# Delaying the issue of the first K tile until VectorE's first constant is written, and letting GpSimd instead of SyncE wait for the output stores

## Chip, cores and metric

The kernel runs on one core of one Trainium2 chip. The metric is the device time of one execution in microseconds (us). A "span" is the length of the profiled part of an execution, from the first to the last instruction of the program on the core; it leaves out what happens around the program and is here 1.7 to 3 us shorter than the device time.

## The reference

Two independent attention decode blocks, A and B, are computed and their outputs concatenated. One block:

```python
# B, Sq, D = 8, 1, 1024 ; H, Sk, Dh = 32, 4096, 128 ; all bf16
q = (x @ wq).reshape(B, Sq, H, Dh).transpose(0, 2, 1, 3)
scores = jnp.einsum("bhqd,bhkd->bhqk", q, k_cache) * (Dh ** -0.5)
p = softmax(scores, axis=-1)
o = jnp.einsum("bhqk,bhkd->bhqd", p, v_cache)
y = o.transpose(0, 2, 1, 3).reshape(B, Sq, H * Dh) @ wo
# ... the same for B; result = concatenate([a, b], axis=-1)
```

There is one query token for each batch entry, so every byte of the K and V caches is read once and used once. The caches, weights and inputs are 1107 MB, and the output is 32 KB.

## The kernel before

All large loads go through a ring of three 8.4 MB slots in SBUF. A plan fixes the order of the loads and the slot of each: `wq` of block A, then K tile 0, then `wq` of block B, then K and V tiles in turn, and the two `wo` at the end. Every large load is issued by SyncE ("sp"), and each waits until the previous tenant of its slot has been used.

```python
plan = [("wq", 0, 1), ("k", 0, 0), ("wq", 1, 2)]          # (kind, number, slot)
for n in range(NQ - 1):
    plan.append(("k", n + 1, (n + 1) % 2))
    plan.append(("v", n, 2))
plan += [("v", NQ - 1, NQ % 2), ("wo", 0, 2), ("wo", 1, (NQ - 1) % 2)]
tenant = [None, None, ("x", 0)]                           # slots 0 and 1 start empty, x is in slot 2
# ...
def load_tiles():
    while issued[0] < len(plan):
        kind, n, w = plan[issued[0]]
        prev = before[issued[0]]                          # the tile that was in this slot
        dep = opUse.get(prev)                             # its last use
        if prev is not None and dep is None:
            return
        # ... dma(to, from_, key, [dep]) by kind ...
        issued[0] += 1
```

The first two loads wait for nothing and are emitted ahead of the block in which the engines branch off to their own streams. Two small loads of `x` (16 KB each) are issued by ScalarE; they wait for `c_oh`, VectorE's first constant. TensorE transposes `x`, and with that and `wq` it computes the queries. After the last store SyncE waits until all the output has landed.

```python
c_oh = add("dve", lambda e: e.tensor_copy(own_h[:], own), [c_own])
# ...
op_x = [dma(x_sb[:, c, :], caches[c][0].rearrange("b s d -> b (s d)"), ("x", 0), [c_oh], "act") for c in range(NC)]
# ... emit_xT: 16 small transposes of x on TensorE ...
op_xT = opUse[("x", 0)] = add("pe", emit_xT, [c_ident, op_x[-1]])
load_tiles()
# ...
P.run("sp", nc.sync, sems, part=(0, 2))
block = es.enter_context(nc.Block())

@block.sync
def _(eng):
    P.run("sp", eng, sems, part=(2, None))
    eng.wait_ge(sems[("out", 0)], counts[("out", 0)])
# ... tensor, scalar, vector ...
@block.gpsimd
def _(eng):
    P.run("pool", eng, sems)                              # writes constants, then has nothing to do
```

## Time and profile before

| | before |
|---|---|
| device time, median of 3 (range) | 2564.32 us (2564.31 to 2564.78) |
| span of the profiled execution | 2563.2 us |
| SyncE's DMA queue (q1) busy | 99.9% of the span |
| bytes read, mean rate | 1107.33 MB, 432 GB/s |
| VectorE (DVE) busy | 85% |

These lines are from the page of the kernel before: the busy time of the engines, the rate of the DMA in 40 equal slices, the busiest queue, the bytes and the engines of the chain that ended last.

```profile
span 2563.2 us, 18707 instructions
...
PE 1122.2 (44%) x7648; PEld 395.1 (15%) x7648; DVE 2173.1 (85%) x1043; ACT 130.0 (5%) x401; POOL 2.6 (0%) x14
...
GB/s 425 427 438 430 437 431 437 431 437 431 436 432 436 431 437 430 438 430 438 430 438 429 438 430 438 429 437 431 437 431 436 432 436 432 434 433 434 433 435 391
...
q1 hardware_dynamic: 19488, 1107.32, 99.9%
...
HBM read 1107.33 MB, written 0.03 MB: 432 GB/s over the span
...
DMA 52%; DVE 28%; issue 16%; PE 4%; another core or an unknown queue 0%; ACT 0%; DVEq 0%; SPq 0%
```

The queue's 99.9% and the even rate say that the 16 DMA engines have work from start to end; counted from the packet records, they are at least 99.4% busy in every stretch of 10 us between 10 and 2550 us. The chain of waits puts 52% on DMA and 28% on VectorE, but that does not make VectorE a second bound. A load waits for a free slot and so for the engine that used it, and the chain follows such a wait even though, by that count, the DMA engines were busy with other loads. The last slice (391) is clearly low: it holds the tail, after the last weights have landed. The first (425) holds the head, before the first bytes arrive; the second, at 427, is nearly as low, and why was not looked into. The packet records show 64 KB packets, 16 at a time, the first of them at 1.84 us; in full flow one takes 2.42 us.

Next, the start in the timeline of the kernel before. The columns are start in us, length in us, engine (a "q" marks work of the engine's sequencer, here the issue of a DMA), source line, operation, output and input, count, and in brackets how long the engine had been idle and what ended it.

```profile
0.81 0.41 SPq L208 DMA_DIRECT2D ring<-in_A_wq_dram  x1
...
1.27 0.42 SPq L208 DMA_DIRECT2D ring<-in_A_k_cache_dram  x1
...
2.29 0.17 DVE L225 CAST own_h<-own_m 128x8 bf16<-128x8 f32 x1 [2.29 <-POOL own_m L212]
...
2.50 0.59 ACTq L208 DMA_DIRECT2D ring<-in_A_x_dram  x1
...
15.97 1.10 PE L450 MATMUL misc<-ident,ring 8*128 8x8 bf16 x16 [15.97 <-DMA ring<-in_B_x_dram]
...
23.23 3.59 PE L284 MATMUL o<-ring,xT 128*8 128x512 bf16 x32 [6.15 <-DMA ring<-in_A_wq_dram]
...
43.72 4.42 DVE L329 TENSOR_TENSOR ring<-ring,qbc 128x8192 bf16<-128x8192 bf16 x1 [10.04 <-DMA ring<-in_A_k_cache_dram]
```

K tile 0 (K0) is issued 0.46 us after `wq`, but the multiply that needs it starts 20.5 us after the first use of `wq` (43.72 against 23.23 us). TensorE has `x` at 15.97 us and then waits 6.15 us for `wq`. The first K multiply waits for K0 itself, until 43.72 us. So `x` is not what the start waits for, and K0's issue at 1.27 us seems far too early to decide anything.

Finally, the instructions of the end barrier of the kernel before, from the listing of that source line. The columns are line, engine, operation, count, least, median and longest duration in ns, and the times in us of the first and last.

```profile
L162 POOLq EVENT_SEMAPHORE  x2: 17/17/17, 2563.0 to 2563.1; - x2
L162 POOLq DRAIN  x1: 349/349/349, 3.8 to 3.8; - x1
...
L162 SPq COMPARE_BRANCH  x1: 33/33/33, 2562.8 to 2562.8; - x1
L162 SPq DRAIN  x1: 7/7/7, 2563.0 to 2563.0; - x1
```

SyncE's branch at 2562.8 is what follows its wait for the output. GpSimd's own drain took place at 3.8 us and lasted 349 ns.

### The profile page before, as it was taken

The page shows a single profiled execution, that of the slowest core. Times are in us where ns is not written, and L with a number is a line of the kernel's source. Part 1 is how long each engine was busy: PE and PEld are TensorE (multiplying, and loading weights), DVE is VectorE, ACT ScalarE, POOL GpSimd, SP SyncE. Part 2 cuts the span into 40 slices and gives each one's busy share as a digit, 9 for nine tenths or more (in the row PEclk, how much of TensorE's full clock was granted, in tenths as well). Part 3 has the DMA queues.
Part 4 walks back from the last instruction along what each step waited for, and adds up shares of the span by engine and source line. Part 5 has one row for each costly group of instructions (what it writes and reads, how often), then busy time and mean ns, then how long its engine had stood idle before and what let it go on. Part 6 is the DMA issues. An engine that isn't in the chain of part 4 may idle for free.

```text
span 2563.2 us, 18707 instructions
## 1 busy us (share of the span) xinstructions
PE 1122.2 (44%) x7648; PEld 395.1 (15%) x7648; DVE 2173.1 (85%) x1043; ACT 130.0 (5%) x401; POOL 2.6 (0%) x14
## 2 busy tenths in 40 slices
PE   2443443443444444444444444443434444434435
PEld 1111111111111111111111111111111111111112
DVE  3898898898898898898898888888988988988983
ACT  1100000000000000000000000000000000000000
POOL 0000000000000000000000000000000000000000
PEclk7666675766667676766767666767767667666667
DMA  9999999999999999999999999999999999999999
GB/s 425 427 438 430 437 431 437 431 437 431 436 432 436 431 437 430 438 430 438 430 438 429 438 430 438 429 437 431 437 431 436 432 436 432 434 433 434 433 435 391
DMA packets 19577, 1107.49 MB, mean 432 GB/s; under 512 B 2224, under 2 KB 2272, under 8 KB 2416
## 3 DMA queue, kind: packets, MB, share of 16 engines
q1 hardware_dynamic: 19488, 1107.32, 99.9%
q8 instruction: 6, 0.10, 0.0%
q10 hardware_dynamic: 80, 0.05, 0.0%
q14 instruction: 3, 0.02, 0.0%
HBM read 1107.33 MB, written 0.03 MB: 432 GB/s over the span
## 4 chain that ended last, share of the span: by engine, by line
DMA 52%; DVE 28%; issue 16%; PE 4%; another core or an unknown queue 0%; ACT 0%; DVEq 0%; SPq 0%
DMA ring<-in_A_k_cache_dram 25%; DMA ring<-in_B_k_cache_dram 25%; DVE ring L329 10%; DVE ring L334 10%; PE red L344 4%; DVE s_sb L352 4%; DVE PM L369 3%; DMA ring<-in_B_wo_dram 1%; DVE rmax L358 1%; DVE rtmp L359 0%; ACT PM L290 0%; DVEq L135 0%; DVE ngm L362 0%; PE proj L432 0%
## 5 line engine op out<-in xcount | busy, mean ns | idle before, releaser
L329 DVE TENSOR_TENSOR ring<-ring,qbc 128x8192 bf16<-128x8192 bf16 x256 | 1131.8, 4421 | 311.3 <-DMA ring<-in_A_k_cache_dram 153.5
L344 PE MATMUL red<-ring,ident 128*128 128x512 bf16 x2048 | 784.0, 552 | 1390.3 <-DVE ring L334 1390.3
L334 DVE TENSOR_TENSOR ring<-ring 128x4096 bf16<-128x4096 bf16 x256 | 582.4, 2275 | 0.0
L344 PEld LDWEIGHTS red<-ring,ident 128*128 128x128 bf16 x2048 | 240.1, 128 | 1842.3 <-DVE ring L334 1492.9
L352 DVE TENSOR_REDUCE s_sb<-red 128x64 f32<-128x1024 f32 x256 | 312.1, 1219 | 3.7 <-PE red L344 3.7
L381 PE MATMUL pv<-ring,PM 128*32 128x512 bf16 x4096 | 274.8, 416 | 4.7 <-DVE PM L369 4.7
L369 DVE TENSOR_TENSOR PM<-pe,own_h 128x2048 bf16<-128x2048 bf16 x64 | 146.2, 2285 | 0.7 <-ACT pe L364 0.7
L381 PEld LDWEIGHTS pv<-ring,PM 128*32 128x32 bf16 x4096 | 104.2, 104 | 188.9 <-issue 116.7
L318 ACT ACTIVATE qbc<-misc 128x128 bf16<-128x128 f32 x64 | 17.8, 278 | 1093.7 <-PE misc L316 1093.7
L364 ACT ACTIVATE pe<-s_sb,ngm 128x256 bf16<-128x256 f32 x64 | 32.6, 509 | 467.4 <-DVE ngm L362 467.4
L389 ACT ACTIVATE accS<-pv 128x512 bf16<-128x512 f32 x64 | 38.2, 597 | 351.2 <-PE pv L381 351.2
L398 PEld LDWEIGHTS o<-accS,E 128*32 128x32 bf16 x1024 | 31.3, 100 | 49.6 <-issue 48.4
L398 PE MATMUL o<-accS,E 128*32 128x32 bf16 x1024 | 38.1, 185 | 0.7 <-ACT accS L389 0.7
L404 ACT ACTIVATE o_sb<-o 32x32 f32 (+1 forms) x64 | 11.9, 186 | 453.4 <-PE o L398 445.3
L358 DVE TENSOR_REDUCE rmax<-s_sb 128x1 f32<-128x256 f32 x64 | 26.9, 420 | 2.2
L437 DVE CAST orow<-proj 40x512 bf16<-40x512 f32 (+1 forms) x2 | 1.1, 554 | 26.1 <-PE proj L432 26.1
L432 PE MATMUL proj<-ring,on_sb 128*8 128x256 bf16 (+1 forms) x192 | 14.8, 387 | 13.6 <-DMA ring<-in_A_wo_dram 7.9
L311 ACT ACTIVATE qst<-qT 128x128 bf16 (+1 forms) x64 | 18.8, 293 | 2.0 <-DVE qT L304 2.0
L304 DVE COPY qT<-misc 128x64 bf16<-128x64 bf16 x8 | 3.5, 436 | 17.2 <-PE misc L300 17.2
L359 DVE TENSOR_SCALAR rtmp<-half,rmax 128x32 f32<-128x32 f32 x64 | 15.5, 241 | 2.3
L362 DVE TRANSPOSE_TENSOR_REDUCE ngm<-rtmp 128x1 f32<-128x32 f32 x64 | 13.6, 212 | 2.2
L316 PE MATMUL misc<-ident,qst 128*128 128x128 bf16 x64 | 14.8, 232 | 0.9 <-ACT qst L311 0.9
(33 smaller groups left out, 63.6 us busy)
## 6 DMA issues: line engine op xcount, KB each, us to landing
ring<-in_B_wo_dram SPq DMA_DIRECT2D x2, 3072.0 KB, 31.4
ring<-in_B_wo_dram SPq DMA_DIRECT2D x1, 1536.0 KB, 38.1
ring<-in_A_k_cache_dram SPq DMA_DIRECT2D x32, 39.9
ring<-in_A_v_cache_dram SPq DMA_DIRECT2D x32, 27.8
ring<-in_B_k_cache_dram SPq DMA_DIRECT2D x32, 39.9
ring<-in_B_v_cache_dram SPq DMA_DIRECT2D x32, 27.8
ring<-in_B_wo_dram SPq DMA_DIRECT2D x1, 512.0 KB, 38.9
out_dram<-orow SPq DMA_DIRECT2D x2, 4.0 KB
```

Of the source, the lines that this page charges most:

```text
L311: return e.activation(qst[:, n % 2, :].rearrange("p (j m) -> p j m", m=MP), from_.unsqueeze(2).to_broadcast([128, HQ, MP]), ACTF.Copy)
L318: opQbc[n] = add("act", lambda e: e.activation(qbc[:, n % 2, :], misc[:, 0:Dh], ACTF.Copy), [opQb[n], _at(opMul, NR * (n - 2) + NR - 1)])
L329: opMul[s] = add("dve", lambda e: e.tensor_tensor(v, v, qbc[:, n % 2, :].unsqueeze(1).to_broadcast([128, CT, Dh]), ALU.mult), [opT[("k", n ...
L334: return add("dve", lambda e: e.tensor_tensor(v[:, :, 0:64], v[:, :, 0:64], v[:, :, 64:128], ALU.add), [opMul[s]])
L344: i = e.matmul(dst, ident[:], v[:, g, :, j, :], start=(j == 0), stop=(j == 3))
L352: opRed[s] = add("dve", lambda e: e.tensor_reduce(s_sb[:, n % 2, r * CT:(r + 1) * CT], red_ps[s % 2][:, :].rearrange("p (t w) -> p t w", w ...
L358: m = add("dve", lambda e: e.tensor_reduce(rmax[:], s_sb[:, n % 2, :], AX.X, ALU.max), [opRed[NR * n + NR - 1]])
L364: opExp[n] = add("act", lambda e, at: e.activation(pe[:], s_sb[:, n % 2, :], ACTF.Exp, bias=ngm[:, n % 2:n % 2 + 1], scale=scale, accum_ou ...
L369: opPM[n] = add("dve", lambda e: e.tensor_tensor(PM[:], pe[:].unsqueeze(2).to_broadcast([128, T, HQ]), own_h[:].unsqueeze(1).to_broadcast( ...
L381: i = e.matmul(pv_ps[32 * q:32 * (q + 1), :], PM[:, t:t + 4, :].rearrange("p t j -> p (t j)"), v[:, t * Dh:(t + 4) * Dh], start=(g == 0), ...
L389: opAcc[n] = add("act", lambda e: e.activation(accS[:], pv_ps[:], ACTF.Copy), [opPV[n], _at(opExt, n - 1)])
L398: x = e.matmul(to, E[:, i, PH - 1 - u:PH - 1 - u + MB], accS[:, i * 128 + H * u:i * 128 + H * (u + 1)], start=(i == 0 and u == 0), stop=(i ...
```

## The change

K0 gets the wait for `c_oh` that the loads of `x` have. That puts its issue after the branch into the engines' own streams, so only `wq` stays ahead of it. The final wait moves from SyncE to GpSimd, which has been idle since the start and collects the end barrier.

```diff
-                dep = opUse.get(prev)
+                dep = c_oh if (kind, n) == ("k", 0) else opUse.get(prev)
...
-        P.run("sp", nc.sync, sems, part=(0, 2))
+        P.run("sp", nc.sync, sems, part=(0, 1))
         block = es.enter_context(nc.Block())
 
         @block.sync
         def _(eng):
-            P.run("sp", eng, sems, part=(2, None))
-            eng.wait_ge(sems[("out", 0)], counts[("out", 0)])
+            P.run("sp", eng, sems, part=(1, None))
...
         @block.gpsimd
         def _(eng):
             P.run("pool", eng, sems)
+            eng.wait_ge(sems[("out", 0)], counts[("out", 0)])
```

## The prediction

> **What bounds the kernel now.** The DMA stream. The queue table of the page has SyncE's queue (q1) busy for 99.9% of the span: 1107.32 MB at 432 GB/s. The costliest groups show VectorE (85% busy, not the limit) idle 311.3 us before the K multiply, mostly for K tiles. SyncE's own waits are for free buffers (V slots 1967.0 us, K slots 436.1 us), but loads are issued well before the stream needs them: K lands 39.9 us and V 27.8 us (median) after issue, while one 8.4 MB tile takes about 19 us at that rate (estimate). So 8 to 20 us of work is always queued. In the packet records the stream runs unbroken from the first packet at about 1.8 us to about 2559 us.
>
> **What the change does.**
> 1. The first K load moves from 1.27 us (timeline) to after VectorE's own_h copy (2.29 us, 0.17 long): about 1.2 us later. The wq load ahead of it still issues at 0.81 us and lands 22.3 us later, so K0 queues with about 20 us to spare and its data still follow wq without a gap. On the critical path: 0.
> 2. K0 now issues in the same moment as ScalarE's x loads (2.50 and 3.12 us), which wait for the same constant. The Trainium skill ("Perfetto Trace Analysis", HWDGE DMA instruction) says an issuer locks the descriptor generator, so one may delay the other by about an issue (0.3 to 0.4 us here). Perhaps x was meant to go ahead of K0. But x has landed by 15.9 us, and the query projection waits for wq until 23.2: 6.2 us of slack. "DMA: Bandwidth & Descriptors" (Queues, rings and completion order) says queues take turns by packet; this trace agrees: x's 2 KB packets ran at 7.3 and 12.2 us between wq's 64 KB packets, so they already pass K0. Worth 0.
> 3. The final wait moves to GpSimd. SyncE's wait ended at 2562.81, its branch and drain were done by 2562.99, GpSimd (which gathers the end barrier) went on at 2563.01, and the last engine left at 2563.19. With GpSimd waiting itself, one hop (0.03 to 0.1 us) goes, but GpSimd's drains took 0.19 and 0.35 us at the start against SyncE's 0.007. Net -0.1 to +0.3 us, all on the critical path.
>
> Bytes, order of loads in SyncE's queue, compute and loops are unchanged.
>
> **Predicted time:** 2564.4 us, range 2562.9 to 2566.0. Faster by over 2%: 0.005; within 2%: 0.99; slower by over 2%: 0.005.
>
> **What the profile should show.**
> - K0's issue at 2.4 to 3.2 us; x issues 0 to 0.5 us later, landing within 1 us of 15.9 or some us earlier; query projection still at about 23.2 us, first K multiply at 43.7 us (within 0.5).
> - q1 still 99.9%, 432 GB/s; VectorE's idle time unchanged.
> - GpSimd waits for the output stores; from their landing to the last instruction 0.3 to 0.7 us, as against 0.4.
>
> **What would make it wrong.** If x had been stuck behind K0's descriptors, it would land several us earlier: still no gain, since wq gates. If the stream ran dry near 21 us, the first K multiply would start late: I expect none. The 16 DMA engines finish the last weights some 2 us apart, so a different spread of small packets could move the end by about 1 us either way. [...] A change of 2% (51 us) would need another DMA rate throughout, which nothing here touches.

## The result, and the profile after

| | before | after |
|---|---|---|
| device time, median of 6 | 2564.48 us | 2564.87 us |
| range of the 6 | 2564.31 to 2564.78 | 2564.4 to 2565.95 |
| span of the profiled execution | 2563.2 us | 2563.0 us |

The ratio is 1.0002 with a 95% interval of 0.9989 to 1.0015. A ratio is the mean time of one kernel's runs over that of the other's of the same rounds, so it is not quite the ratio of the medians. The change made no difference that can be told from noise: the medians differ by 0.39 us, and the interval is about 3 us wide on either side. The spans of the six executions of the changed kernel were 2562.7 to 2563.2 us; what device time has beyond the span varied from 1.7 to 2.9 us among them, so most of the spread lies outside the span.

The same lines of the page, of the kernel after:

```profile
span 2563.0 us, 18707 instructions
...
PE 1120.7 (44%) x7648; PEld 394.1 (15%) x7648; DVE 2172.8 (85%) x1043; ACT 129.8 (5%) x401; POOL 2.5 (0%) x14
...
GB/s 425 427 438 430 437 431 437 431 437 431 437 431 436 432 436 431 435 433 435 432 436 431 436 431 437 431 436 432 434 434 434 433 433 435 433 434 434 434 434 392
...
q1 hardware_dynamic: 19488, 1107.32, 99.9%
...
HBM read 1107.33 MB, written 0.03 MB: 432 GB/s over the span
```

The first ten slices agree to the digit, although K0 is issued later in the first of them. The start, in the timeline of the kernel after:

```profile
0.80 0.40 SPq L208 DMA_DIRECT2D ring<-in_A_wq_dram  x1
...
2.28 0.17 DVE L225 CAST own_h<-own_m 128x8 bf16<-128x8 f32 x1 [2.28 <-POOL own_m L212]
...
2.48 0.35 SPq L208 DMA_DIRECT2D ring<-in_A_k_cache_dram  x1
2.49 0.59 ACTq L208 DMA_DIRECT2D ring<-in_A_x_dram  x1
...
15.87 1.11 PE L450 MATMUL misc<-ident,ring 8*128 8x8 bf16 x16 [15.87 <-DMA ring<-in_B_x_dram]
...
23.15 3.19 PE L284 MATMUL o<-ring,xT 128*8 128x512 bf16 x32 [6.17 <-DMA ring<-in_A_wq_dram]
...
43.47 4.42 DVE L329 TENSOR_TENSOR ring<-ring,qbc 128x8192 bf16<-128x8192 bf16 x1 [10.30 <-DMA ring<-in_A_k_cache_dram]
```

K0 is issued 1.21 us later, and `x`, the query projection and the first K multiply start where they did, within 0.25 us. And the end barrier of the kernel after:

```profile
L162 POOLq EVENT_SEMAPHORE  x2: 17/17/17, 2562.8 to 2562.9; - x2
...
L162 POOLq COMPARE_BRANCH  x1: 33/33/33, 2562.6 to 2562.6; - x1
L162 POOLq DRAIN  x1: 41/41/41, 2562.8 to 2562.8; - x1
```

The branch that follows the wait is now GpSimd's, and its drain takes 41 ns, against 7 ns for SyncE's before.

The same end in finer numbers, read from the instruction records of the traces (us from the start of each span; the two halves of the change by themselves are experiments told below):

| | before | after | K0's wait alone | final wait alone |
|---|---|---|---|---|
| last issue of an output store ends | 2561.651 | 2561.442 | 2561.216 | 2561.332 |
| final wait is over | 2562.813 | 2562.602 | 2562.384 | 2562.502 |
| last engine leaves | 2563.193 | 2563.018 | 2562.765 | 2562.918 |
| last issue to end of the wait | 1.162 | 1.160 | 1.168 | 1.170 |
| end of the wait to the last engine | 0.380 | 0.416 | 0.381 | 0.416 |

GpSimd notices the landed output about as soon as SyncE does (1.16 to 1.17 us either way), and then the end takes 0.036 us longer. From the branch to GpSimd's collecting of the barrier it was 0.165 us to the drain, 0.007 for SyncE's drain and 0.026 from there to GpSimd before; after, it is 0.148 us to GpSimd's own drain, 0.041 for the drain and 0.044 behind it. So the drain is longer, and the step from one engine to the other did not become a saving. That is the whole cost of the change that the traces show: 0.0014% of the time.

### The profile page after: what moved, and what is told of

The parts are those of the page before. It is cut to its first block, busy times and chain, and to the rows that moved or that the text cites. A ratio compares the mean times of both kernels' runs of the same rounds, so it can differ in the third digit from the quotient of the medians.

```text
span 2563.0 us, 18707 instructions
## 1 busy us (share of the span) xinstructions
PE 1120.7 (44%) x7648; PEld 394.1 (15%) x7648; DVE 2172.8 (85%) x1043; ACT 129.8 (5%) x401; POOL 2.5 (0%) x14
## 3 DMA queue, kind: packets, MB, share of 16 engines
q1 hardware_dynamic: 19488, 1107.32, 99.9%
## 4 chain that ended last, share of the span: by engine, by line
DMA 52%; DVE 28%; issue 16%; PE 4%; another core or an unknown queue 0%; ACT 0%; DVEq 0%; SPq 0%; POOL 0%; POOLq 0%
DMA ring<-in_A_k_cache_dram 25%; DMA ring<-in_B_k_cache_dram 25%; DVE ring L329 10%; DVE ring L334 10%; PE red L344 4%; DVE s_sb L352 4%; DVE PM L369 3%; DMA ring<-in_B_wo_dram 2%; DVE rmax L358 1%; DVE rtmp L359 0%; ACT PM L290 0%; DVEq L135 0%; PE o L284 0%; DVE ngm L362 0%
## 5 line engine op out<-in xcount | busy, mean ns | idle before, releaser
L329 DVE TENSOR_TENSOR ring<-ring,qbc 128x8192 bf16<-128x8192 bf16 x256 | 1131.1, 4418 | 311.2 <-DMA ring<-in_A_k_cache_dram 158.0
```

The lines of the kernel that those rows point to most:

```text
L329: opMul[s] = add("dve", lambda e: e.tensor_tensor(v, v, qbc[:, n % 2, :].unsqueeze(1).to_broadcast([128, CT, Dh]), ALU.mult), [opT[("k", n ...
```

## The experiments

The theory is that the DMA stream is the bound, that it has about 20 us of `wq` to read before it needs K0's descriptors, and that `x` is not what the start waits for. So moving K0's issue by 1.2 us is free, and only the tail could change. The rivals are that the two halves have effects that cancel; that a delay at the start costs in proportion to its length; and that `x` was being held up. All seven kernels were correct in all their runs. The first four ran on one chip and the other three on another, each set beside nine runs of the kernel before on the same chip.

### K0's wait alone

```diff
 # against the kernel after: SyncE makes the final wait again
         def _(eng):
             P.run("sp", eng, sems, part=(1, None))
+            eng.wait_ge(sems[("out", 0)], counts[("out", 0)])
...
             P.run("pool", eng, sems)
-            eng.wait_ge(sems[("out", 0)], counts[("out", 0)])
```

> Half of the change: K0 waits for VectorE's constant, SyncE keeps the final wait. Theory (the DMA stream is the bound and K0 is queued some 20 us early): K0's issue at about 2.48 us, first K multiply at 43.5 to 43.7 us, span 2562.7 to 2563.5 us, time within 0.1% of before; the tail from the end of the final wait to the last instruction 0.38 us as in before. Rival A (K0's later issue slows the start, which the final wait's move hides): 1 us or more over before in the span, with the first K multiply later than 44.5 us. Rival B (x was stuck behind K0 and gains): x's first matmul several us before 15.9 us.

Measured: 2564.80 us median of 5 against 2564.75 us of before, ratio 1.0001 (0.9987 to 1.0014), span 2562.8 us. K0 was issued at 2.49 us, `x`'s first matmul came at 16.03 us and the first K multiply at 43.34 us; the end took 0.381 us. The first K multiply came 0.16 us before the range that was expected (43.5 to 43.7). So this half is neutral by itself, and neither rival A nor rival B holds.

### The final wait alone

```diff
 # against the kernel before
         def _(eng):
             P.run("sp", eng, sems, part=(2, None))
-            eng.wait_ge(sems[("out", 0)], counts[("out", 0)])
...
             P.run("pool", eng, sems)
+            eng.wait_ge(sems[("out", 0)], counts[("out", 0)])
```

> The other half: GpSimd makes the final wait, K0 issues at about 1.27 us as before. Theory: the tail from the end of the final wait to the last instruction is 0.41 to 0.43 us (after: 0.416, before: 0.380), the wait ends 1.16 us after the end of the last output issue as in both; span 2562.7 to 2563.5, time within 0.1%. Rival (a GpSimd wait wakes late, and K0's part made up for it): the wait ends over 1.4 us after the last output issue, or the tail is over 0.6 us.

Measured: 2564.81 us median of 5 against 2564.75 us, ratio 1.0001 (0.9987 to 1.0014), span 2562.9 us. The wait ended 1.170 us after the last issue, and the end took 0.416 us, the same to the nanosecond as in the full change. The halves do not hide each other.

### K0 held back until x has been transposed

```diff
-                dep = c_oh if (kind, n) == ("k", 0) else opUse.get(prev)
+                dep = op_xT if (kind, n) == ("k", 0) else opUse.get(prev)
```

> K0 is held back further, until TensorE has transposed x: issue near 17.0 us instead of 2.48. Theory (only an empty queue costs; wq keeps the DMA engines busy to about 22 us): no loss, first K multiply at 43.3 to 44.2 us, span 2562.7 to 2563.9. Rival (what counts is how long K0 is held back): a loss in proportion, 5 to 15 us.

Measured: 2564.83 us median of 4 against 2564.75 us, ratio 1.0000 (0.9985 to 1.0015), span 2563.1 us. From the timeline of this run:

```profile
16.99 0.35 SPq L208 DMA_DIRECT2D ring<-in_A_k_cache_dram  x1
...
43.49 4.42 DVE L329 TENSOR_TENSOR ring<-ring,qbc 128x8192 bf16<-128x8192 bf16 x1 [9.97 <-DMA ring<-in_A_k_cache_dram]
```

A delay of 15.7 us against before (1.27 to 16.99), thirteen times that of the change, cost nothing, and K0 arrived as before. Cost in proportion to the delay is ruled out.

### K0 held back until the queries have been computed

```diff
-                dep = c_oh if (kind, n) == ("k", 0) else opUse.get(prev)
-                if prev is not None and dep is None:
+                dep = opQ.get((0, 1)) if (kind, n) == ("k", 0) else opUse.get(prev)
+                if (prev is not None or (kind, n) == ("k", 0)) and dep is None:
...
         make_q(0)
+        load_tiles()
```

(The wait is on the last matmuls that read `wq`, those of the second half of the columns; the text below says the first half, while its time is that of the edit.)

> K0, and with it every later load, waits until the query projection of the first half has read wq: issue near 28 us, when wq has landed and nothing is queued. Theory: the DMA engines idle from about 22 us to about 29 us and the whole loss is that gap: span and time 5.5 to 9 us longer (about 2571.5 us), first K multiply later by the same, end no earlier. Rival (there is slack later, since VectorE is busy for 85% only, so that the late start is caught up): under 2 us longer.

Measured: 2573.63 us median of 4 (2572.61 to 2574.17) against 2564.75 us, ratio 1.0033 (1.0018 to 1.0049), span 2571.5 us, that is 8.5 us over that of after. From the timeline of this run:

```profile
28.98 0.35 SPq L208 DMA_DIRECT2D ring<-in_A_k_cache_dram  x1
...
29.38 0.42 SPq L208 DMA_DIRECT2D ring<-in_B_wq_dram  x1
...
52.06 4.42 DVE L329 TENSOR_TENSOR ring<-ring,qbc 128x8192 bf16<-128x8192 bf16 x1 [18.39 <-DMA ring<-in_A_k_cache_dram]
```

The busy times by stretch show the hole. The columns are the stretch, its length, the busy time of five engines with their counts, the clock granted to TensorE, the share of the DMA engines that was busy (counted by packet, so it can pass 1 a little) and GB/s. First this run, then the kernel after:

```profile
20.00:40.00 20.00, 7.26 (x97) 3.05 (x97) 1.74 (x4) 5.48 (x11) 0.00 (x0) 0.86 0.54 217
```

```profile
20.00:40.00 20.00, 6.57 (x97) 2.94 (x97) 1.74 (x4) 5.48 (x11) 0.00 (x0) 0.82 0.99 427
```

In the packet records nothing larger than 4 KB was in flight on SyncE's queue from 22.57 to 29.95 us, a hole of 7.38 us common to all 16 engines. They don't stop and start together: the last packets of `wq` end between 22.07 and 22.57 us and the first ones of K0 start between 29.95 and 30.35, so the mean pause of an engine is 7.85 us. On the restart the first packets took 2.87 to 3.34 us instead of 2.42, on average 0.72 us more. These add up to 8.57 us, against 8.59 us by which the first K multiply and 8.49 us by which the end came later than in the kernel after. (The first packets of the program are as slow: in the kernel before they took 2.51 to 3.34 us, 0.73 us more on average.) My estimate of about 7 us left the restart out. Nothing was made up in the remaining 2500 us, though VectorE is busy for only 85% of the time: a hole in the stream is paid in full. The same records give the true deadline. The first engine ran dry at 22.07 us and K0's first packet came 0.97 us after its issue, so K0 may be issued as late as about 21.1 us (an estimate from those two readings; no run issued K0 between 17.0 and 29.0 us). The change used 1.2 us of about 20 us.

### wq held back as well

```diff
-                dep = c_oh if (kind, n) == ("k", 0) else opUse.get(prev)
+                dep = c_oh if (kind, n) in (("wq", 0), ("k", 0)) else opUse.get(prev)
...
-        P.run("sp", nc.sync, sems, part=(0, 1))
+        P.run("sp", nc.sync, sems, part=(0, 0))
...
-            P.run("sp", eng, sems, part=(1, None))
+            P.run("sp", eng, sems, part=(0, None))
```

> The same wait put before the first load of all: wq waits for VectorE's constant as well, so it issues near 2.48 us instead of 0.80. Theory: nothing is queued ahead of it, so the delay of 1.68 us is paid in full: first packet near 3.5 us instead of 1.83, first K multiply 1.4 to 2.0 us later, span 1.2 to 2.2 us longer than after (2564.2 to 2565.2 us). Rival (slack of the pipeline swallows any small start delay): span within 0.5 us of after.

Measured: 2566.28 us median of 5 (2566.16 to 2566.55) against 2564.99 us (2564.56 to 2566.13, 9 runs), ratio 1.0004 (0.9991 to 1.0018). The interval by itself does not separate them; the spans do, better. They were 2564.4 to 2564.7 us in all five runs, while eight of the nine of before lay between 2562.8 and 2563.2 us (the ninth was 2564.4). From the timeline of this run:

```profile
2.49 0.40 SPq L208 DMA_DIRECT2D ring<-in_A_wq_dram  x1
2.50 0.59 ACTq L208 DMA_DIRECT2D ring<-in_A_x_dram  x1
...
2.95 0.42 SPq L208 DMA_DIRECT2D ring<-in_A_k_cache_dram  x1
...
45.34 4.42 DVE L329 TENSOR_TENSOR ring<-ring,qbc 128x8192 bf16<-128x8192 bf16 x1 [10.36 <-DMA ring<-in_A_k_cache_dram]
```

The first packet of `wq` ran at 3.55 us instead of 1.83, the first K multiply came 1.87 us later than in the kernel after (45.34 against 43.47) and the profiled span was 1.7 us longer, so the delay of 1.69 us was paid in full. The same wait for the same constant is free on the second load and costs its whole length on the first, because nothing is queued ahead of the first.

### x issued at once

```diff
-        op_x = [dma(..., ("x", 0), [c_oh], "act") for c in range(NC)]
+        op_x = [dma(..., ("x", 0), [], "act") for c in range(NC)]
```

> The changed kernel, with the two x loads issued at once instead of after VectorE's constant: near 0.8 us. Theory (x lands early either way and wq gates the query projection): x's first matmul at 3 to 9 us instead of 15.9, second wq load issued as much earlier, but query projection still near 23.1 us, first K multiply at 43.3 to 44 us, span 2562.7 to 2563.8: no gain. Rival (x's landing gates the start, and the change meant to help it): first K multiply and the end 1 us or more earlier.

Measured: 2564.73 us median of 4 against 2564.99 us, ratio 0.9998 (0.9983 to 1.0013). From the timeline of this run:

```profile
0.80 0.60 ACTq L208 DMA_DIRECT2D ring<-in_A_x_dram  x1
...
11.00 1.12 PE L450 MATMUL misc<-ident,ring 8*128 8x8 bf16 x16 [11.00 <-DMA ring<-in_B_x_dram]
12.14 0.33 SPq L208 DMA_DIRECT2D ring<-in_B_wq_dram  x1
...
23.10 3.58 PE L284 MATMUL o<-ring,xT 128*8 128x512 bf16 x32 [10.99 <-DMA ring<-in_A_wq_dram]
...
43.33 4.43 DVE L329 TENSOR_TENSOR ring<-ring,qbc 128x8192 bf16<-128x8192 bf16 x1 [9.79 <-DMA ring<-in_A_k_cache_dram]
```

`x` came 4.9 us earlier than in the kernel after, and TensorE simply waited longer for `wq` (10.99 us instead of 6.17). The rival that `x` gates the start falls. My figure for `x` missed: I expected 3 to 9 us and it was 11.00. The packets say why. In the kernel before, the two loads of `x` and their two semaphore writes ran at 7.28, 9.78, 12.20 and 14.73 us, each one 64 KB packet of `wq` (2.42 us) apart; issued at once, the first load and its semaphore write ran ahead of `wq` at 1.76 and 1.85 us, but the second pair still ran at 7.32 and 9.82 us. Why no packet of `x` ran at about 4.9 us, between the first two rounds of `wq`, was not looked into.

The profiled execution of this kernel had a span of 2564.3 us; its other three had 2562.7 to 2563.1. In the long one the final wait ended 2.47 us after the last issue (2561.398 to 2563.863) instead of 1.16. An instruction fetch of 16 KB ran from 2561.20 to 2562.18 us, beside the stores; in the profiles of before and after the last such fetch came only after the end. Four store packets ran right behind it (2562.17 to 2562.34 us), and it was the last four completions of the stores that came late, 0.2 us apart (2563.25 to 2563.84). One execution of the kernel before also had a span of 2564.4 us, so a long end does not need the edit. That the fetch is the cause is likely from this, but was not tested.

### Work for GpSimd behind its final wait

```diff
+        spare = sb("spare", [128, 128], BF16)
...
             eng.wait_ge(sems[("out", 0)], counts[("out", 0)])
+            eng.memset(spare[:], 0.0)
```

> The changed kernel, with GpSimd writing 128x128 bf16 zeros to a spare tile after its final wait. Theory (GpSimd's drain is as long as its own unfinished work, 0.04 us when it has none, which is why the forecast from the drains of the start was too high): the drain at the end takes 0.1 to 0.4 us in place of 0.041, and the tail from the end of the wait to the last instruction 0.5 to 0.9 us in place of 0.416. Rival (the drains of the start were long for another reason): the drain stays under 0.06 us though the write is there.

Measured: 2564.98 us median of 4 against 2564.99 us, ratio 1.0000 (0.9985 to 1.0016), profiled span 2563.3 us. From the listing of the barrier's line in this run:

```profile
L162 POOLq DRAIN  x1: 271/271/271, 2562.8 to 2562.8; - x1
```

The drain took 271 ns instead of 41, as expected of a drain that waits for its engine's own unfinished work: the write is recorded from 2562.783 to 2562.987 us (such records of GpSimd are rough), and the drain ended at 2563.036 us. The whole tail was expected to take 0.5 to 0.9 us from the end of the wait. No branch was recorded after the wait here, so that interval can't be read in the same way. From the last completion of a store (2562.734) to the last engine (2563.264) it was 0.53 us, against 0.44 us in the kernel after (2562.578 to 2563.018): 0.09 us more. In the kernel after the branch comes 0.024 us behind the last completion; with the same here, the tail from the end of the wait was about 0.51 us (an estimate), at the lower edge. The tail lengthened less than the drain did (0.23 us), because the drain began earlier: 0.03 us after the last completion instead of 0.17. So the recorded length of a drain is not by itself what it adds to the end.

### No faster version

Nothing here points to a version that beats both kernels. As counted above, the stream is full from its first packet at 1.84 us almost to the last weights at about 2559 us. What lies outside it, the 1.8 us before the first packet and the 3.8 us from the last weights to the end, is about 5.6 us in 2563, 0.2%.

## Why the prediction was right

- **The bound.** It held that the DMA stream alone sets the time. The runs show it at the start from both sides. The late K0 (a pause of 7.85 us for each engine and a slow restart cost 8.5 us) and the late `wq` (1.7 us cost 1.7 us) interrupt the stream and are paid in full; K0 at 2.48 and at 16.99 us does not, and is free. That 8 to 20 us of loads are queued at all times later in the run is still an estimate; what the records show there is that the DMA engines stay busy. VectorE's idle time before the K multiplies stayed the same, as forecast (311.3 and 311.2 us).
- **K0's later issue: 0.** This was right. The issue moved to 2.48 us (forecast 2.4 to 3.2), the first K multiply stayed at 43.47 us (forecast 43.7 within 0.5), and "about 20 us to spare" agrees with the estimated deadline of about 21.1 us.
- **Two issuers at the same moment.** The prediction took from the Trainium skill ("Perfetto Trace Analysis", HWDGE DMA instruction) that an issuer locks the descriptor generator, and worked out that one may delay the other by 0.3 to 0.4 us. No delay was seen: SyncE's issue of K0 is recorded from 2.483 to 2.833 us and ScalarE's issue of `x` from 2.487 to 3.076, so they overlap for all but 4 ns of the first. The issue of `x` took 0.589 us, as it did in the kernel before with SyncE idle. This term was offered as possible and worth 0, so it changed nothing.
- **x.** It was right that `x` already passed K0 and that `wq` is what the queries wait for: 15.87 against 15.97 us, and the projection at 23.15. The packet turns that "DMA: Bandwidth & Descriptors" (Queues, rings and completion order) describes are what the records show from 7.3 us on, one turn for each 2.42 us packet.
- **The tail: -0.1 to +0.3 us.** It was +0.036 us, inside, but with neither term as forecast. The saving of one hop (0.03 to 0.1 us) did not come: from the end of the drain to GpSimd's next step it took 0.026 us before and takes 0.044 us now. And GpSimd's drain was mis-sized. The prediction used 0.19 and 0.35 us, read behind memory writes at the start; at the end GpSimd was idle and its drain took 0.041 us. The last experiment shows the difference: 0.271 us with a write in front of it. The two terms as forecast give about +0.08 to +0.31 us (an estimate from the prediction's own figures), so it is the margin at the lower end of the range that held the result.
- **The total.** 2564.4 us was forecast (2562.9 to 2566.0) and 2564.87 us was measured. The difference of 0.39 us between the medians of before and after is not attributed: 0.036 us of it is seen in the trace, and the rest is within what runs of one kernel differ by (2564.4 to 2565.95 us).

## What to carry to other kernels

When one queue is busy for 99.9% of the span, ask of any moved issue or wait only whether the queue can run empty because of it: by the estimate above, an issue may move freely up to about one first-packet lag (here 1 us) before the work ahead of it ends. Past that point the time was lost for good in the two cases tried here, the pause before K0 and the late `wq`. The same wait cost its whole length on the first load of this program and nothing on the second. Read the length of a drain at a place where its engine has as little to finish as in the place you forecast.

## What the Trainium skill lacked or had wrong

- "Perfetto Trace Analysis", HWDGE DMA instruction: it says the descriptor generator is locked for exclusive use while it generates, and that the lock wait is inside the recorded interval. Here two issues from SyncE and ScalarE overlapped from 2.487 to 2.833 us and neither got longer (0.350 and 0.589 us; alone they took 0.349 us, at 16.99 us in the run with K0 behind the transposes, and 0.589 us). A lock held for a small part of each issue is not excluded.
- "DMA: Bandwidth & Descriptors", Specifications: it gives about 0.6 us as the first-byte latency of this path. Here the first 64 KB packet ran 0.97 to 1.06 us after the start of the issue when the queue was empty (0.805 to 1.844, 28.98 to 29.95, 2.491 to 3.551 us). The start of a packet's record may not be its first byte, so the two need not be the same quantity.
- "DMA: Bandwidth & Descriptors", Specifications and Bandwidth: it lists a fabric ceiling of 435 GB/s and an HBM limit of about 358 GB/s for a core, and its text lets the second one bind for HBM loads, although it also reports 425 GB/s measured for a core alone. This core read HBM at 432 GB/s over the whole span, so in a run of one core like this one the page's sentence that the lower limit binds does not hold; its own 425 GB/s is near.
- No page found gives the cost of restarting an emptied stream: the first packets after a pause took 2.87 to 3.34 us instead of 2.42, on average 0.72 us more.
- No page found says how the length of a GpSimd drain depends on the engine's unfinished work: here it took 0.041 us with the engine idle and 0.271 us right behind a 128x128 bf16 write.
